# Output product of the first parity as seven half products, tiles that land in place, and places of their own for 130 tasks

## The chip, the cores and the metric

The kernel runs on one core of a Trainium2 chip. A core has TensorE (PE; its weight loads are listed as PEld), VectorE (DVE), ScalarE (ACT), GpSimd (POOL) and SyncE (SP), which here only issues DMA transfers. Each engine works through its own list of instructions in order. The metric is the time of one execution on the device in microseconds (us), the median of the runs; a profile is one execution of its own, taken with the hardware profiler.

## The reference

x has 2048 tokens of 640 numbers, all in float32. Two branches are mixed by a gate for each token: attention over 8 positions at distance 2 (32 heads of 20), and a dense layer with Mish.

```python
qkv = x @ wqkv                                   # 640 -> 3*640
logits = einsum("bhsd,bhswd->bhsw", q, kg) * DH**-0.5   # kg: k at s, s-2, ..., s-14
attn = softmax(where(mask, logits, -1e9))
o = einsum("bhsw,bhswd->bhsd", attn, vg)
a = o.reshape(B, S, 640) @ wo                    # the output product, 640 -> 640
h = x @ w1 + b1                                  # 640 -> 1728
b = (h * tanh(softplus(h))) @ w2                 # Mish, 1728 -> 640
g = sigmoid((x * gate_w).sum(-1, keepdims=True))
return g * a + (1 - g) * b
```

## The kernel before

**Tiles.** Everything is held transposed: features on the 128 partitions, 512 tokens along a row. The 2048 tokens are split by parity P (0, 1), and each parity into two blocks of 512, so tb = 0, 1 are the first parity and tb = 2, 3 the second. 640 features are five chunks (kc for those that are summed over, dc for those of the result).

**Precision.** A float32 tile becomes a pair of two fp32r tiles, a high part (ScalarE, line 400) and a low part, the difference (VectorE or GpSimd, line 403; `split`). A product of two pairs, `mm3` (lines 441 to 443), is three matmuls of 128x128 by 128x512. A tile is loaded into a staging buffer (rings `raw`, `hb`, `z`), then split into a buffer of the ring `pair` (`load_pair`).

**Half products.** A 2x2 block of products needs eight; the scheme of Strassen and Winograd does it in seven, with sums of the operands made ahead and sums of the results made behind. `quad` does the first layer of the MLP so: for two chunks of features and two token blocks, half products go into five PSUM banks, ScalarE copies one bank into another (line 887) as the start of the next sum, and VectorE closes (line 920). `mlp2` does the second layer with seven products a, b, c, e, g, d, f, each in seven steps over kc (step number 7k + kc for the k-th of them, 49 in all). The sums of w2 are made by `sums_of_w2` and kept in DRAM (s), the sums of activations by DMA with accumulation.

**Attention** is VectorE's work: eight units (parity by four groups of eight heads); products (lines 494, 532) and sums of 128x2560, softmax with ScalarE, and a transposed o of 128x640, which is stored to DRAM (`o<-ot`) and read again as chunks of 128 features.

**Output product** (`wo_out`, lines 1288 and after). For tb 0 and 1 the gated rows b of the MLP (`wo_row`, the gate's product on line 1127) are copied into a bank by ScalarE as its start (line 1274), five `mm3` over kc follow (`wo_bank`), ScalarE copies the bank out (line 1281), and the block is stored: 2 blocks x 5 dc x 5 kc x 3 = 150 matmuls. For tb 2 and 3 the first three kc come first, VectorE adds the result to b (line 1284), and the last two kc come at the end, again with a start and a copy by ScalarE. wo is loaded by `load_wo`, all of it, at step 26 of `mlp2`.

**What sets the order.** The program first records all work as tasks (`add`), each with an engine (or "ANY": VectorE or GpSimd), a duration, what it waits for, the buffers that it takes and holds, and a rank. `Plan.run` then plays them through and emits each engine's instructions in the order in which that play starts them: for each engine that is idle, of those tasks which are ready and whose buffers are free, the one with the lowest rank, then the earliest `need` (the place on TensorE of what waits for it, less `HOP` for each stage between), then the one recorded first. Rings hand out their buffers in the order of recording. FRONT lists the stages of the first part in the order in which they are recorded (Q units of qkv and attention, T quads, F and M rows of the first layer, S sums of w2, and the loads), BACK those which are recorded at a step of `mlp2` (2S5 is S with 5 at step 2; W is `load_wo`, G the gate's rows, P a row b). Loads of `mlp2` are recorded three steps ahead.

## Time and profile before

| | |
|---|---|
| time before, median of 3 runs | 624.56 us (624.12 to 627.35) |
| the profiled execution's own time | 628.4 us |
| its span | 626.3 us |
| mean granted clock of TensorE | 0.999 |
| DMA | 149.47 MB, mean 239 GB/s over the span |
| HBM read, written | 85.61 MB, 60.69 MB |

The span is what the profiler saw from the first to the last instruction; the execution's own time has some us around it. The stages by their places: the first layer and qkv until about 400 us, the seven products of the second layer from there to about 550, the output product to the end, with attention beside all of them until 580 us. Lines named "wait" give the engine, its line, what it waited for, the total, the number of times and the longest; rows of a timeline give start, duration, engine, line, operation, out<-in and, in brackets, idle time ahead and what ended it. Durations of matmuls are longer than their spacing, since they overlap. Names with a number less are tiles: `bank` PSUM, `pair`, `raw`, `hb`, `z` the rings, `kvq` rooms of attention of which some are reused, `act` and `actt` activations of the first layer in DRAM and their sums, `in_...` the inputs.

### The profile page before, as it was taken

To read this page: it belongs to the slowest core of one execution; us is meant where nothing else is said; L and a number is where in the kernel's file an instruction comes from. 1 tells how busy PE (TensorE), PEld (TensorE's weight loads), DVE (VectorE), ACT (ScalarE), POOL (GpSimd) and SP (SyncE) were. 2 spreads that over 40 slices of the span, in tenths; PEclk is the share of its full clock that TensorE was granted. 3 is DMA by queue.
4 is the path that set the end of the run, shared out by engine and by line. 5 is a ranking of instruction groups with operands and counts; after the bars stand their busy time and mean duration, and the time that the engine had idled before them with its cause. 6 is when DMAs were issued, how large, how long until landed. Compare 5 with 4: busy or idle time off the path is not lost.

```text
span 626.3 us, 8954 instructions
## 1 busy us (share of the span) xinstructions
PE 617.0 (99%) x2717; PEld 509.8 (81%) x2717; DVE 565.2 (90%) x581; ACT 384.2 (61%) x851; POOL 255.3 (41%) x250
## 2 busy tenths in 40 slices
PE   9999999998999999999999999989999999999997
PEld 6888888887888788888888888877888788888885
DVE  6899999998999999999999989989999999999630
ACT  6666765776496676766676535185858456575234
POOL 2563266546464445354456646441312431503000
PEclk9999999999999999999999999999999999999999
DMA  8866389998999699979997988689998687875404
GB/s 307 254 200 197 93 235 279 262 255 225 333 265 290 148 289 308 231 203 256 282 295 214 313 211 229 201 239 281 341 332 297 199 259 233 260 252 172 138 1 169
DMA packets 100609, 149.47 MB, mean 239 GB/s; under 512 B 11456, under 2 KB 47296, under 8 KB 100528
## 3 DMA queue, kind: packets, MB, share of 16 engines
q1 hardware_dynamic: 93456, 136.05, 67.6%
q0 software_dynamic: 7104, 12.85, 13.4%
q8 instruction: 21, 0.34, 0.2%
q14 instruction: 28, 0.23, 0.1%
HBM read 85.61 MB, written 60.69 MB: 234 GB/s over the span
## 4 chain that ended last, share of the span: by engine, by line
PE 87%; DVE 5%; DMA 4%; issue 2%; POOL 1%; ACT 1%; SPq 1%; DVEq 0%; POOLq 0%; ACTq 0%
PE bank L443 28%; PE bank L441 28%; PE bank L442 28%; DMA act<-z 1%; PE bank L587 1%; POOL pair L403 1%; DVE pr L494 1%; DVE pair L403 1%; DMA raw<-act 1%; PE bank L383 1%; PE bank L1208 1%; DMA hb<-act 1%; PE bank L1207 1%; DMA z<-act 0%; DVE pr L542 0%
## 5 line engine op out<-in xcount | busy, mean ns | idle before, releaser
L442 PE MATMUL bank<-pair 128*128 128x512 f32 (+2 forms) x812 | 314.8, 388 | 2.1 <-DVE pair L403 2.0
L441 PE MATMUL bank<-pair 128*128 128x512 f32 (+2 forms) x812 | 314.4, 387 | 0.0
L443 PE MATMUL bank<-pair 128*128 128x512 f32 (+2 forms) x812 | 314.3, 387 | 0.0
L403 POOL TENSOR_TENSOR pair<-raw,pair 128x512 fp32r<-128x512 f32 (+3 forms) x104 | 130.9, 1270 | 190.9 <-DVE side L536 47.3
L442 PEld LDWEIGHTS bank<-pair 128*128 128x128 f32 x812 | 152.5, 188 | 32.8 <-DVE pair L403 3.0
L441 PEld LDWEIGHTS bank<-pair 128*128 128x128 f32 x812 | 152.5, 188 | 30.6 <-ACT bank L887 0.5
L443 PEld LDWEIGHTS bank<-pair 128*128 128x128 f32 x812 | 152.6, 188 | 30.0 <-POOL pair L403 0.2
L400 ACT ACTIVATE pair<-raw 128x512 fp32r<-128x512 f32 (+3 forms) x198 | 117.0, 611 | 44.4 <-DMA raw<-act 19.7
L532 DVE TENSOR_TENSOR pr<-kvq,side 128x2560 f32<-128x2560 f32 x32 | 90.2, 2820 | 1.0
L497 DVE TENSOR_REDUCE lg<-pr 128x128 f32<-128x2560 f32 x32 | 90.1, 2817 | 0.7
L494 DVE TENSOR_TENSOR pr<-kvq,side 128x2560 f32<-128x2560 f32 x32 | 90.1, 2815 | 0.5
L403 DVE TENSOR_TENSOR pair<-raw,pair 128x512 fp32r<-128x512 f32 (+3 forms) x94 | 62.7, 690 | 7.3 <-ACT pair L400 7.0
L593 ACT ACTIVATE kvq<-bank 128x320 f32<-128x320 f32 x64 | 27.9, 437 | 46.8 <-PE bank L443 46.8
L542 DVE TENSOR_TENSOR pr<-pr 128x1280 f32<-128x1280 f32 x32 | 48.7, 1522 | 0.8
L400 ACT ACTIVATE pair<-hb 128x512 fp32r<-128x512 f32 (+2 forms) x40 | 24.7, 617 | 19.8 <-DMA hb<-actt 11.7
L403 POOL TENSOR_TENSOR pair<-hb,pair 128x512 fp32r<-128x512 f32 x12 | 15.6, 1301 | 42.3 <-PE bank L443 12.5
L887 ACT ACTIVATE bank<-bank 128x512 f32<-128x512 f32 x36 | 21.0, 584 | 16.0 <-PE bank L443 15.9
L441 PE MATMUL bank<-kvq,pair 128*128 128x512 f32 x72 | 28.3, 393 | 1.6 <-ACT bank L887 1.6
L443 PE MATMUL bank<-kvq,pair 128*128 128x512 f32 x72 | 28.3, 393 | 0.1
L442 PE MATMUL bank<-kvq,pair 128*128 128x512 f32 x72 | 28.1, 390 | 0.0
L740 POOL TENSOR_TENSOR raw<-raw 128x256 f32<-128x256 f32 (+1 forms) x24 | 20.4, 875 | 17.8 <-DVE side L536 8.2
L683 POOL DMA_DIRECT2D actt<-actt x26 | 22.4, 862 | 12.7 <-DVE pair L403 7.8
(125 smaller groups left out, 598.7 us busy)
## 6 DMA issues: line engine op xcount, KB each, us to landing
raw<-in_w SPq DMA_DIRECT2D x34, 256.0 KB, 4.8
raw<-actt SPq DMA_DIRECT2D x30, 256.0 KB, 4.0
raw<-in_wq SPq DMA_DIRECT2D x30, 248.0 KB, 3.5
raw<-in_x SPq DMA_DIRECT2D x29, 256.0 KB, 5.4
actt<-hb SPq DMA_DIRECT2D x28, 256.0 KB, 4.0
act<-z SPq DMA_DIRECT2D x24, 256.0 KB, 6.4
actt<-z SPq DMA_DIRECT2D x24, 256.0 KB, 6.0
raw<-act SPq DMA_DIRECT2D x23, 256.0 KB, 4.7
```

What stands on the lines that cost most here:

```text
L400: a = add("ACT", act_ns(n), lambda: A.activation(hi(), raw(), AF.Copy), after, rank=rank, take=take, hold=hold, kind="hi")
L403: return (V if e == "DVE" else G).tensor_tensor(lo(), raw(), hi().bitcast(F32), op=OP.subtract)
L441: nc.tensor.matmul(ps, ah, bh, start=first, stop=False, skip_group_check=more)
L442: nc.tensor.matmul(ps, ah, bl, start=False, stop=False, skip_group_check=more)
L443: nc.tensor.matmul(ps, al, bh, start=False, stop=last, skip_group_check=more)
L494: return V.tensor_tensor(pr, window(kv, s0, 0), qs[:, :, None, :].to_broadcast([128, 2, W, QF]), op=OP.mult)
L497: return V.tensor_reduce(lg_w[:, s0:s0 + 2], pr.rearrange("p s w (h d) -> p s w h d", d=DH), op=OP.add, axis=AX.X)
L532: return V.tensor_tensor(pr.rearrange("p s w (h d) -> p s w h d", d=DH), vw, pw[:, :, :, :, None].to_broadcast([128, 2, W, HQ, DH]), op=OP ...
L542: step("DVE", 1495, lambda: V.tensor_tensor(pr[:, :, 0:4], pr[:, :, 0:4], pr[:, :, 4:8], op=OP.add))
L593: a = add("ACT", 330, lambda: A.activation(kv[:, 7 + s], ps.t[:, QF:3 * QF].rearrange("p (a b) -> p a b", a=2), AF.Copy), [done] + before, ...
L683: return add("POOL", 1200, lambda: G.dma_start(out=blk[key][:rows], in_=src(), accum_op=OP.add, max_dma_last_dim=2048), after, rank=-0.5, ...
L887: return add("ACT", 590, lambda: A.activation(to.t, of.t, AF.Copy), after, rank=-0.6, take=[to], hold=[of], kind=kind)
```

## The change

1. *Output product of tb 0 and 1.* For dc = 0, 1 and dc = 2, 3 a new `wo_quad` does what `quad` does: 18 `mm3` with seven half products over kc 0 to 3 and the rest for kc 4, in place of 20; dc = 4 stays as it was. That is 46 `mm3` in place of 50, so 138 matmuls in place of 150. ScalarE copies banks three times in each quad; VectorE adds each of six bank results to its row b (`plus_bank`), where ScalarE made a start and a closing copy before.
2. *Sums ahead.* `sums_of_wo` (two times four sums of 128x256, three tiles stored) and `sums_of_o` (two times four sums of 128x512, four tiles stored) are recorded at steps 13, 21 and 23 of `mlp2`, kept in DRAM (`wt`, `os`) and loaded again for the quads. Three kinds of sums of o land in room of attention's `kvq0` after its unit 6 (`wo_sums`).
3. *Landing in place.* `Landing` with `inner=True` has a DMA write straight into the low half of a pair; ScalarE makes the high half from it, and the low half is overwritten by the difference. The activations and s of `mlp2`, o, os and wt land so.
4. *Rings and order.* `hb` has two buffers, `z` four. FRONT and BACK stand in another order; M for tb 2 and 3 is recorded at step 0, G at 35, and `load_wo` in three parts within `wo_out`. The constants of `Plan` change.
5. *Places of their own.* Five tables give single tasks, by their number, another key, a delay before they count as ready, another need, another rank, or one engine: 130 tasks in all.
6. *The host* lays wo out in blocks of 128 in the order of ORDER.

```diff
-SIZES = {"pair": 23, "home": 6, "raw": 9, "hb": 3, "z": 3}
+SIZES = {"pair": 23, "home": 6, "raw": 9, "hb": 2, "z": 4}
-BACK = "1M2 1M3 43P4 0S6 2S5 31P1 26W 22G 35P0"
-EARLY_S = 4000
+BACK = "23O0 13V0 0M2 7S6 21O1 2S5 35G 0M3 21V1"
+EARLY_S = 0
...
+HELD_BACK = """6:8079 17:633 18:4827 54:264 56:1872 184:656 185:632 187:1661 207:335 224:722 319:252 339:1148 354:778 384:1945
...
-    NEAR, TURN, PATIENCE, HOP, STAY, HELD = 4500, 2200, 11000, 3712, 3000, 24502
+    NEAR, TURN, PATIENCE, HOP, STAY, HELD = 3564, 1936, 11000, 6531, 3456, 14750
...
-            t.key = (t.rank, i)
+            t.key = (t.rank, i + moved.get(i, 0))
+            t.late += held.get(i, 0)
+            t.bias, t.only, t.turn = needed.get(i, 0), engine.get(i, 0), t.rank + ranked.get(i, 0)
...
-    def load_pair(src, eng, n=512, rank=SOON, drank=0.0, after=(), wide=False, home=None, cols=1):
-        raw, p = stage(wide), home or pair_buf()
+    class Landing:
+        def __init__(self, inner, n, home=None, wide=True):
+            self.p, self.n, self.inner = home or pair_buf(), n, inner
+            self.raw = None if inner else stage(wide)
+            self.take = [self.p if inner else self.raw]
...
+        def at(self, rows=slice(0, 128), a=0, b=None):
+            b = self.n if b is None else b
+            return self.p.t[rows, 1, a:b].bitcast(F32) if self.inner else self.raw.t[rows, a:b]
...
-        acts = [load_pair(lambda P=P: blk[of, P, kc], "ANY", wide=i > 2, after=done[of, P, kc]) for P in range(2)]
+        acts = [load_pair(lambda P=P: blk[of, P, kc], "ANY", after=done[of, P, kc], inner=True) for P in range(2)]
...
+    def sums_of_wo(m):
...
+        s1 = sum_into((r[2], 0), (r[1], 0), (r[0], 0), OP.subtract, [d0, d1], 256, take=[r[2]], rank=NEXT)
...
+        for i in (1, 2, 3):
+            wt_in[m, i] = [dma(lambda i=i: wt_d[m, i], lambda i=i: r[i].t, ends[i], rank=0.7, hold=[r[i]])]
+    def sums_of_o(kp):
...
+        s1 = sum_into((a22, 0), (a21, 0), (a22, 0), OP.add, a21.ready + a22.ready, 512, rank=NEXT)
+        s3 = sum_into((a21, 0), (a11, 0), (a21, 0), OP.subtract, [s1] + a11.ready, 512, rank=NEXT)
+        s2 = sum_into((a11, 0), (a22, 0), (a11, 0), OP.subtract, [s3], 512, rank=NEXT)
+        s4 = sum_into((a12, 0), (a12, 0), (a11, 0), OP.subtract, [s2] + a12.ready, 512, rank=NEXT)
+        for i, raw, t in ((1, a22, s1), (2, a11, s2), (4, a12, s4), (3, a21, s3)):
+            os_in[kp, i] = [dma(lambda i=i: os_d[kp, i], lambda raw=raw: raw.t, [t], rank=0.7, hold=[raw])]
...
+    def wo_quad(P, m, OX, OS, bs):
...
+        p1 = mm(one, of(xs(t0, 0), 0, 0), [], True, True, [one], "open")
+        p5 = mm(five, of(s(1), 2, 0), [p1], True, True, [five])
+        c2 = copy(two_, one, [p1])
+        plus_bank(t0, fb, five, [p5])
+        plus_bank(t1, fb, five, [p5])
+        p6 = mm(two_, of(s(2), 2, 256), [p5, c2])
+        p2 = mm(one, of(xs(t0, 1), 0, 256) + [(OX[t0, 4], R[3], 256)], [p6, c2], False, True)
+        plus_bank(t0, fa, one, [p2], True)
+        c3 = copy(three, two_, [p6])
+        p7 = mm(two_, of(s(3), 1, 0), [p2, c3])
+        c4 = copy(four, two_, [p7], "shut")
+        p3 = mm(three, of(s(4), 1, 256) + [(OX[t0, 4], R[3], 384)], [p7, c3], False, True)
+        plus_bank(t0, fb, three, [p3], True)
+        p4 = mm(two_, of(xs(t1, 1), 3, 0) + [(OX[t1, 4], R[3], 256)], [p3, c4], False, True)
+        plus_bank(t1, fa, two_, [p4], True)
+        p8 = mm(four, [(OX[t1, 4], R[3], 384)], [p4, c4], False, True)
+        plus_bank(t1, fb, four, [p8], True)
     def wo_out():
+        load_wo(0)
+        OX, OS = wo_sums(0)
+        load_wo(1)
+        bs = {(tb, dc): b for tb in (0, 1) for dc, b in enumerate(wo_rows(tb))}
+        for m in range(2):
+            wo_quad(0, m, OX, OS, bs)
+        load_wo(2)
+        OX.update({(1, kc): b for kc, b in wo_tokens(1, (0, 2)).items()})
         for tb in (0, 1):
-            ot = wo_tokens(tb, range(KC))
-            bs = wo_rows(tb)
-            for dc in range(KC):
-                wo_bank(tb, dc, bs[dc], ot, True, True)
+            wo_bank(tb, KC - 1, bs[tb, KC - 1], {kc: OX[tb, kc] for kc in range(KC)}, True, True)
```

The order of the instructions moves on every engine. Three places follow. The first is ScalarE in the quad that stands near 146 us of the profile before (hb and z are rows of Mish, lg the logits of attention). Before:

```order
L519 ACTIVATE lg_223<-lg_223 128x256
L400 ACTIVATE pair_1535<-raw_1441 128x512
L400 ACTIVATE pair_1545<-raw_1483 128x128
L695 ACT_TABLE_LOAD
L695 ACTIVATE hb_1547<-bank2_65,bias_77 128x512
L698 ACTIVATE hb_1547<-hb_1547 128x512
L887 ACTIVATE bank6_69<-bank3_66 128x512
```

And after the change:

```order
L576 ACTIVATE lg_223<-lg_223 128x256
L752 ACT_TABLE_LOAD
L752 ACTIVATE hb_1556<-bank3_66,bias_77 128x512
L752 ACTIVATE z_1550<-z_1550,bias_77 128x512
L439 ACTIVATE pair_1569<-raw_1398 128x512
L944 ACTIVATE bank6_69<-bank5_68 128x512
L439 ACTIVATE pair_1582<-raw_1416 128x128
```

The split of 128x128 stood ahead of the table load, the Mish and the bank copy, and stands behind them now; one of the two other splits stands between Mish and copy.

The second place is SyncE's list at the first steps of the second layer (act21 are activations of product b, h2 and h3 the last rows of the first layer on their way through DRAM, s5 and s6 sums of w2). Before:

```order
L409 DMA h2_196<-pair_3833 32x2x128
L409 DMA h2_196<-pair_3833 32x2x128
L409 DMA h3_197<-pair_3840 32x2x128
L409 DMA h3_197<-pair_3840 32x2x128
L409 DMA raw_3896<-act11_1_6_98 128x512
L409 DMA s5_188<-raw_3823 128x128
L409 DMA hb_3899<-act21_0_2_101 128x512
L409 DMA pair_3833<-h2_196 64x512
L409 DMA raw_3915<-act21_0_0_99 128x512
```

(The eight stores stand in one block; the last two of each four are shown.) And after:

```order
L448 DMA pair_3919<-act21_0_2_101 128x512
L448 DMA pair_3922<-act21_1_2_108 128x512
L448 DMA h2_196<-pair_3844 32x2x128
L1050 DMA hb_3928<-in_w2 64x384
L1050 DMA hb_3928<-in_w2 64x384
L448 DMA s6_189<-raw_3842 128x128
L448 DMA h2_196<-pair_3844 32x2x128
L448 DMA s5_188<-raw_3597 128x128
L448 DMA h2_196<-pair_3844 32x2x128
L448 DMA pair_3963<-act21_0_3_102 128x512
L448 DMA pair_3967<-act21_1_3_109 128x512
```

The eight stores are spread between loads, most of product b's activations stand ahead of the later ones, and they go into pair buffers.

The third place is SyncE's list within product c (actt2 are its activations, s its weights, o attention's result, b a finished row of the MLP). Before:

```order
L409 DMA raw_4235<-actt2_1_3_151 128x512
L409 DMA raw_4249<-actt2_0_4_145 128x512
L409 DMA raw_4257<-actt2_1_4_152 128x512
L1025 DMA hb_4259<-s4_187 128x256
L1025 DMA hb_4259<-s5_188 128x256
L409 DMA raw_4269<-actt2_1_5_153 128x512
```

And after:

```order
L448 DMA raw_4212<-o0_190 128x512
L1078 DMA pair_4225<-s4_187 128x256
L1078 DMA pair_4225<-s5_188 128x256
L448 DMA wt0_2_247<-raw_4080 128x512
L448 DMA pair_4244<-actt2_0_4_145 128x512
L448 DMA pair_4247<-actt2_1_4_152 128x512
L448 DMA pair_4262<-actt2_0_5_146 128x512
L448 DMA pair_4270<-actt2_1_5_153 128x512
L448 DMA raw_4275<-o1_191 128x512
```

Loads of o and a store of a sum of wo now stand between the loads of product c; that store waits for VectorE's sum, and the loads of steps 4 and 5 stand behind it.

More of the change, by code (lines that the diff above doesn't have):

```diff
@@ L38 @@
 KEPT = "".split()
+DEEP = 3
 AHEAD = 1.0
@@ L177, in run @@
                         continue
-                    t = min(fit, key=(lambda t: (t.rank, t.need if t.need is not None and e in ("DVE", "POOL", "ACT") and self.ORDERED else 1e9, t.key)))
+                    t = min(fit, key=(lambda t: (t.turn, (t.need if t.need is not None and e in ("DVE", "POOL", "ACT") and self.ORDERED else 1e9) + t.bias,
+                                            t.key[1])))
                     if t.both:
@@ L996, in load_low_w @@
[L996 to L1003 removed]
+                nc.sync.dma_start(to.at(slice(a, a + FR)), src())
@@ L1377 @@
     mlp2(mid, listed)
-    if not WO:
-        load_wo()
     wo_out()
```

242 lines of the change are left out of this document (178 added, 64 removed), and 15 rows, old and new, of tables (HELD_BACK, NEEDED, RANKED).

## The prediction

> **What bounds the kernel now.** First the page's first part, the busy time of each engine. One line carries it:
>
> ```profile
> PE 617.0 (99%) x2717; PEld 509.8 (81%) x2717; DVE 565.2 (90%) x581; ACT 384.2 (61%) x851; POOL 255.3 (41%) x250
> ```
>
> TensorE is busy 99% of the span, so a matmul that goes away is worth its spacing. A busy row is longer than that spacing, since matmuls overlap; it is read from the timeline, from two starts that stand 90 matmuls apart:
>
> ```profile
> 509.40 0.39 PE L441 MATMUL bank<-pair 128*128 128x512 f32 x1
> 529.80 0.39 PE L441 MATMUL bank<-pair 128*128 128x512 f32 x1
> ```
>
> 20.40/90 = 0.2267 us each, at a granted clock of 1.00. Second, the waits of TensorE:
>
> ```profile
> PE bank L442 <- DVE pair L403: 2.0, 1, 2.0
> PE bank L441 <- ACT bank L887: 1.6, 1, 1.6
> PE bank L383 <- DVE lg L379: 1.2, 1, 1.2
> PE bank L1208 <- DVE pair L1013: 0.2, 1, 0.2
> ```
>
> That is all: 5.0 us, and 1.2 of it is the start. After a gap the next matmuls also start slowly; the chain of the end has six more such pieces outside the two long waits, with 0.40 to 0.50 where 0.23 is usual, first and last:
>
> ```profile
> 179.17 0.50 PE bank L441
> 501.39 0.47 PE bank L1208
> ```
>
> They hold about 1.5 us together (six times about 0.25). Third, who feeds TensorE. The windows give, after the stretch and its length, the busy time of PE, PEld, DVE, ACT and POOL, then the clock, the busy share of the DMA engines and GB/s:
>
> ```profile
> 430.00:480.00 50.00, 50.00 (x222) 41.43 (x221) 48.16 (x63) 35.77 (x74) 9.12 (x8) 1.00 1.02 334
> 430.00:580.00 150.00, 149.74 (x660) 123.56 (x659) 146.00 (x184) 95.86 (x194) 38.63 (x33) 1.00 0.82 264
> 580.00:610.00 30.00, 30.00 (x134) 24.86 (x133) 13.99 (x22) 8.32 (x14) 0.00 (x0) 1.00 0.22 68
> ```
>
> VectorE has only 150 − 146.0 = 4.0 us free in the 150 us from 430, yet TensorE waits 0.26 us there. From 430 to 480 the DMA engines are full as well. From 580 VectorE has 30 − 14.0 = 16 us to spare. So **TensorE bounds, with VectorE right behind it**, and any forecast is a question of whether VectorE can take more.
>
> **The sum.** All terms are made on the profiled execution, 628.4 us (span 626.3, and 2.1 around it); it lies 3.8 above the median of 624.56, with the same clock. I take it that the differences carry over, so the forecast on the profile's scale is 3.8 higher.
>
> 1. *Twelve matmuls go.* Two quads of 18 half or single products stand for two times 20 in tb 0 and 1; 46 products of three matmuls in place of 50. 12 × 0.2267 = **−2.7**. This is the surest term.
>
> 2. *The wait at 146 us.* ScalarE's timeline:
>
> ```profile
> 143.10 0.31 ACT L400 ACTIVATE pair<-raw 128x128 fp32r<-128x128 f32 x1 [2.34 <-DMA raw<-in_w]
> 143.43 1.28 ACT L695 ACT_TABLE_LOAD   x1
> 144.73 0.69 ACT L695 ACTIVATE hb<-bank,bias 128x512 f32<-128x512 f32 x1
> 145.98 0.58 ACT L887 ACTIVATE bank<-bank 128x512 f32<-128x512 f32 x1
> 146.61 0.50 PE L441 MATMUL bank<-kvq,pair 128*128 128x512 f32 x1 [1.59 <-ACT bank L887]
> ```
>
> (The last row is TensorE's.) A small split waits 2.34 us for its weights at the head of ScalarE's in-order queue; behind it stand a table load, the Mish and the bank copy that TensorE needs. In the new order this split stands behind the bank copy, and the table load and the Mish need not wait for it. The copy then comes up to 2.34 us earlier, more than the 1.59 that TensorE lost: **−1.6**. Next late there: the Mish needs a free hb buffer, of which there are two in place of three, so it waits for an earlier store.
>
> 3. *The wait at 411 us.* Four engines carry it:
>
> ```profile
> 395.98 5.60 SPq L409 DMA_DIRECT2D h<-pair  x8
> 403.69 0.53 SPq L409 DMA_DIRECT2D raw<-act  x1
> 408.11 0.63 ACT L400 ACTIVATE pair<-raw 128x512 fp32r<-128x512 f32 x1 [2.16 <-DMA raw<-act]
> 409.70 0.56 DVE L978 SCALAR_TENSOR_TENSOR pair<-raw,pair 128x384 fp32r<-128x384 f32 x1 [2.72 <-ACT pair L977]
> 412.44 0.69 DVE L403 TENSOR_TENSOR pair<-hb,pair 128x512 fp32r<-128x512 f32 x1
> 413.78 0.50 PE L442 MATMUL bank<-pair 128*128 128x512 f32 x1 [1.98 <-DVE pair L403]
> ```
>
> Eight stores of the last rows of mlp1 hold SyncE's queue for 5.60 us; the loads behind them are issued late (403.69), ScalarE splits late, VectorE stands idle for 2.72 us and then works off a heap. In the new order the activations of product b are issued ahead of these stores and between them, straight into pair buffers: **−2.0**. What is late next are the stores themselves, and their loads back: the last rows of mlp1 now come between the loads of product b, and a load that stands behind a store waits 0.7 us (5.60/8), not 5.6.
>
> 4. *Six more bank copies by ScalarE.* They stand on TensorE's path in a quad. The price of such copies so far:
>
> ```profile
> L887 ACT ACTIVATE bank<-bank 128x512 f32<-128x512 f32 x36 | 21.0, 584 | 16.0 <-PE bank L443 15.9
> ```
>
> 36 copies and one wait of 1.6 us: 6/36 × 1.6 = **+0.3**; bounds 0 (each hidden behind the next half product) and 6 × 0.58 = 3.5. ScalarE itself, with 61%, loses the seeds and closing copies of tb 0 and 1; two more table loads (1.28 each, above) are hidden there.
>
> 5. *VectorE's added work.* By the counts of instructions it has 18 more of 128x512, 6 more of 128x256 and two fewer of 128x384. Their prices:
>
> ```profile
> 557.95 1.29 DVE L1127 TENSOR_TENSOR kvq<-kvq,pair 128x512 f32<-128x512 f32 x2
> 559.16 0.69 DVE L403 TENSOR_TENSOR pair<-z,pair 128x512 fp32r<-128x512 f32 x1
> L960 DVE TENSOR_TENSOR raw<-raw 128x256 f32<-128x256 f32 x5 | 2.1, 411 | 0.0
> ```
>
> Start to start a 512 costs (559.16 − 557.95)/2 = 0.605, so 18 × 0.605 + 6 × 0.411 − 2 × 0.56 (the row at 409.70) = 12.2 us. About 6.3 of it are early sums in products c to g (seven of 512 by 0.605, five of 256 by 0.411); most of the rest are the twelve closings. Cover: the 4.0 us free from 430 to 580, the 2.72 at 409.70, and 16 us after 580. Attention would finish some 5.5 us later (12.2 − 6.7), which the 16 can hold. Bounds 0 and 12.2. I take **+0.5**, a quarter of the one wait for VectorE of 2.0 that the kernel shows, since the early sums have no due time at TensorE and can be put behind the splits; but the sums' stores can't be put behind: SyncE waits for a sum with a store of wt at the head of its queue, and behind it stand activations of product c.
>
> 6. *More transfers in the full stage.* Between the first load of product c and that of g there are 11 more transfers of 256 KB (five stores of wt, three loads and one store of o and its sums, two loads of wo), 2.88 MB; at 334 GB/s (row 430 to 480) 8.6 us. For it: gate rows and most of wo are loaded later than before, and tiles landing in place are asked for earlier. Bounds 0 and 8.6; I take one of the eleven as late, 8.6/11 = **+0.8**, nearer to 0 because the row shows all 222 matmuls in 50 us without a pause although the share is 1.02 already. The Trainium skill, "DMA: Bandwidth & Descriptors", section "Where 436 GB/s comes from", puts the limit between HBM and one core at about 358 GB/s and that of the fabric at 435; by the second this term would be nothing, by the first the upper bound would be an estimated 8.1 us. That 334 comes with a share of 1.02 speaks for the first. What is late next is wo itself: its loads now fall between 480 and 580, where the DMA engines have been busy for 0.72 of the time:
>
> ```profile
> 480.00:580.00 100.00, 99.74 (x440) 82.13 (x439) 97.85 (x122) 60.08 (x121) 29.51 (x26) 1.00 0.72 229
> ```
>
> So there is room for them: 28 us of full transfer in these 100 us.
>
> 7. *Landing in place itself* moves no work between engines: the same splits, read from the pair's low half. Its price is that a pair buffer is held through the transfer; 0, hidden by the three steps of loads ahead, else part of 6. The sums of o land in kvq0, whose room is free only when attention's seventh unit has ended; if VectorE is late, so are they, which is again B.
>
> Sum: −2.7 − 1.6 − 2.0 + 0.3 + 0.5 + 0.8 = −4.7, **619.9 us** (623.7 on the profile's scale).
>
> **The rivals.**
>
> *B: VectorE takes over as the pace.* Its free 6.7 us are used, the other 5.5 are on TensorE's path because splits come behind sums and closings: −2.7 − 3.6 + 0.3 + 5.5 = −0.5, **624.1**. For it: 146 of 150 us busy. Against it: what is added is not itself needed soon, and attention can slip into the 16 us. Here it also falls if the waits of 2 and 3 only move. It decides against a gain of 0.5% from 2.9 us unhidden on.
>
> *C: slower, by late transfers at the head of VectorE's queue.* In products c and e the eleven transfers make tiles late; VectorE works in order, so each late tile stops all behind it, its spare time is lost to such waits, and all of the 12.2 are on the path: −6.0 + 12.2 = +6.2, **630.8**. It decides from 9.1 us unhidden (6.0 + 3.1). For it: the share of 1.02, and the 2.72 us at 409.70, which are such a wait. Against it: no wait of TensorE from 430 to 480.
>
> *D: VectorE and GpSimd in each other's way.* The rows:
>
> ```profile
> L403 DVE TENSOR_TENSOR pair<-raw,pair 128x512 fp32r<-128x512 f32 x75 | 50.7, 695 | 5.5 <-ACT pair L400 5.2
> L403 DVE TENSOR_TENSOR kvq<-raw,kvq 128x512 fp32r<-128x512 f32 x5 | 6.4, 1280 | 0.1
> ```
>
> The same split took 1280 ns in five cases, 585 more. GpSimd gets 14 more elementwise operations of 512; if each held up one of VectorE's, 14 × 0.585 = 8.2 on top of B: −0.5 + 8.2 = +7.7, **632.3**. The mean of 695 over 75 says that the order mostly keeps them apart. The Trainium skill, "SBUF — State Buffer", section "Who interferes with whom", says that only the port pair which these two share causes contention, as an exclusive lock; the 1280 agrees, the 695 shows it avoided.
>
> **How the numbers follow.** About 0.5% (3.1 us: 621.4 and 627.7) is what a measurement here can tell from no change. Forecast 0.56, the only case that is faster; B 0.27, the same; C 0.14 and D 0.03, slower. The low end: terms 4 to 6 at nothing (−1.6), the 0.2 of L1208 and the 1.5 of slow starts gone, gives 616.6, and 0.4 for the fastest run's distance from the median: 616.2. The high end: B with the 2.7 us at 409.70 not won back for VectorE, 626.8. C and D, 0.17, are left out.
>
> **What would show it.** In the changed profile: 2705 matmuls or so; no wait for a bank copy of 1.6 near 146 us; no wait for VectorE near 411; DVE's 128x512 operations still near 690 ns; VectorE's last attention product near 584 in place of 578, with the last matmul 4.7 us earlier. B shows as several waits of TensorE for splits by VectorE between 430 and 580; C as VectorE idle behind ScalarE and DMA in products c and e; D as a mean far above 690. The forecast is wrong if the waits of TensorE, 5.0 us now, do not fall below about 3.

## The result, and the profile after

The changed kernel takes **640.87 us** (median of 6 runs, 637.57 to 642.00); the kernel before took 624.34 us beside it (6 runs, 623.56 to 627.35). The ratio is **1.0233, 95% interval 1.0209 to 1.0258**: slower, where 619.9 was forecast and 626.8 was the upper end. The profiled execution took 641.11 us, with a span of 639.4 and a mean granted clock of 0.991 (before 628.4, 626.3 and 0.999).

The page's busy times:

```profile
PE 619.5 (97%) x2705; PEld 509.5 (80%) x2705; DVE 586.5 (92%) x602; ACT 388.6 (61%) x855; POOL 291.6 (46%) x269
```

The twelve matmuls are gone (2705), yet TensorE's share fell from 99% to 97%: it waits. VectorE is busy for 21.3 us more, GpSimd for 36.3 us more (19 more instructions). The waits of TensorE, as total, times and longest:

```profile
PE bank L499 <- POOL pair L442: 6.0, 1, 6.0
PE bank L498 <- ACT kvq L1156: 2.6, 1, 2.6
PE bank L500 <- DVE pair L442: 1.5, 2, 0.9
PE bank L422 <- DVE lg L418: 1.2, 1, 1.2
...
PE bank L500 <- POOL pair L442: 0.9, 1, 0.9
...
PE bank L498 <- ACT bank L944: 0.7, 2, 0.4
```

The two long waits of before (2.0 for a split by VectorE, 1.6 for ScalarE's bank copy) are not among them. In their place stand one of 6.0 us for a split by *GpSimd* and one of 2.6 us for ScalarE's bank copies. The windows (busy time of PE, PEld, DVE, ACT and POOL, then clock, DMA share, GB/s) say where:

```profile
430.00:480.00 50.00, 50.00 (x222) 41.43 (x221) 48.20 (x58) 32.33 (x63) 18.20 (x18) 1.00 0.97 325
480.00:550.00 70.00, 70.00 (x311) 57.89 (x310) 68.22 (x78) 43.94 (x86) 28.95 (x23) 1.00 0.94 307
560.00:570.00 10.00, 4.01 (x13) 2.95 (x12) 6.27 (x11) 2.64 (x6) 8.62 (x2) 0.79 0.91 330
580.00:610.00 30.00, 30.00 (x134) 24.68 (x133) 29.14 (x41) 10.34 (x19) 5.12 (x4) 1.00 0.55 178
```

From 430 to 550, where the prediction looked for trouble, TensorE runs without a pause beside full DMA engines and a VectorE that is busy for 116.4 of 120 us. Then, from 560 to 570, it does 13 matmuls in place of 44, GpSimd is busy for 8.62 us with two instructions, and the clock falls to 0.79.

**The stall at 561.** The timelines of VectorE, GpSimd and TensorE there (start, duration, engine, line, operation):

```profile
556.56 1.88 DVE L442 TENSOR_TENSOR pair<-pair 128x512 fp32r<-128x512 f32 x3
...
564.98 1.29 DVE L442 TENSOR_TENSOR kvq<-kvq 128x512 fp32r<-128x512 f32 x2
572.54 0.69 DVE L1466 TENSOR_TENSOR z<-bank,z 128x512 f32<-128x512 f32 x1 [6.27 <-PE bank L500]
...
559.62 9.01 POOL L442 TENSOR_TENSOR pair<-pair 128x512 fp32r<-128x512 f32 x2 [18.93 <-DMA o<-ot]
...
561.07 0.39 PE L498 MATMUL bank<-pair 128*128 128x512 f32 x1
567.44 0.79 PE L499 MATMUL bank<-pair 128*128 128x512 f32 x1 [5.99 <-POOL pair L442]
568.03 0.63 PE L500 MATMUL bank<-pair 128*128 128x512 f32 x1
568.46 0.63 PE L498 MATMUL bank<-pair 128*128 128x512 f32 x1
568.89 0.63 PE L499 MATMUL bank<-pair 128*128 128x512 f32 x1
```

From 556.56 to 566.27 VectorE runs a train without a gap: sixteen operations, all with both operands in SBUF (the memory that holds the tiles, beside PSUM with its banks), one every 0.605 us. GpSimd begins a split of 128x512 in the middle of it, at 559.62. Such a split lies at about 1.3 us elsewhere; this one ends at 567.39 (it is the first of the two in the row, 7.78 us by the chain), 1.12 us after the train. It is as if GpSimd had stood still until VectorE let go. TensorE needs this split and waits 5.99 us; VectorE, at the end of its train, then waits 6.27 us for TensorE. And after the wait TensorE's matmuls start 0.43 us apart in place of 0.23, for some 5 us.

**The wait at 418.** ScalarE, then TensorE:

```profile
417.98 1.28 ACT L752 ACT_TABLE_LOAD   x1
419.28 0.72 ACT L752 ACTIVATE pair<-pair,bias 64x512 f32<-64x512 f32 x1
420.03 0.63 ACT L755 ACTIVATE pair<-pair 64x512 f32<-64x512 f32 x1
420.56 2.02 ACT L1156 ACTIVATE kvq<-bank 128x512 f32<-128x512 f32 x4
...
421.19 0.50 PE L498 MATMUL bank<-pair 128*128 128x512 f32 x1 [2.60 <-ACT kvq L1156]
...
424.13 0.63 PE L498 MATMUL bank<-pair 128*128 128x512 f32 x1
424.55 0.63 PE L499 MATMUL bank<-pair 128*128 128x512 f32 x1
```

Product a is done at 418.6, and its banks must be copied out before product b's next sum can begin. Ahead of those copies on ScalarE stands the Mish of the last 64 rows of the first layer, with a table load: 2.6 us. These rows came back from DRAM late, since their eight stores now lie between loads:

```profile
406.51 0.32 SPq L448 DMA_DIRECT2D h<-pair  x1
...
411.24 1.58 SPq L448 DMA_DIRECT2D h<-pair  x3
...
413.97 1.14 SPq L448 DMA_DIRECT2D pair<-h  x2
```

**By stretches.** The table takes, from the matmuls' start times, all distance between neighbours beyond 0.2267 us; so it holds waits and slow matmuls together (us; early matmuls of 496 or 498 columns stand closer, hence the negative sums).

| | 0–12 | 12–145 | 145–300 | 300–430 | 430–480 | 480–550 | 550–580 | 580–end | sum |
|---|---|---|---|---|---|---|---|---|---|
| before | 2.9 | −1.4 | 1.3 | 1.4 | 0 | 0.7 | 0 | 0 | 4.9 |
| after | 3.4 | 1.1 | 1.6 | 4.3 | 0 | 0 | 10.4 | 0.2 | 20.9 |

The difference of 16.0, less 2.7 for twelve matmuls, is 13.3; the span grew by 13.1, since what follows the last matmul became 0.2 us shorter. (The medians stand 16.5 apart and the ratio gives 14.5; the profiled execution of before, with 628.4 us, lay above all six runs.) 10.4 of it lies between 550 and 580: the wait of 6.0 at 561, the slow matmuls behind it, and a wait of 1.1 at 557 whose cause the trace does not name.

### The profile page after: what moved, and what is told of

It is laid out like the page before. It is cut to its first block, busy times and chain, and to the rows that moved or that the text cites. A ratio compares the mean times of both kernels' runs of the same rounds, so it can differ in the third digit from the quotient of the medians.

```text
span 639.4 us, 9048 instructions
## 1 busy us (share of the span) xinstructions
PE 619.5 (97%) x2705; PEld 509.5 (80%) x2705; DVE 586.5 (92%) x602; ACT 388.6 (61%) x855; POOL 291.6 (46%) x269
## 3 DMA queue, kind: packets, MB, share of 16 engines
q0 software_dynamic: 7104, 12.85, 13.3%
## 4 chain that ended last, share of the span: by engine, by line
PE 51%; DVE 9%; DMA 3%; issue 1%; POOL 1%; ACT 1%; SPq 1%; DVEq 0%; POOLq 0%; ACTq 0%
PE bank L499 17%; PE bank L500 17%; PE bank L498 17%; DVE lg L554 2%; DVE pr L551 2%; DVE pr L589 1%; DMA pair<-act 1%; POOL pair L442 1%; DVE pr L599 1%; SPq L448 1%; DMA s<-raw 1%; PE bank L1258 1%; PE bank L1257 0%; DMA pair<-h 0%; DVE pr L600 0%
## 5 line engine op out<-in xcount | busy, mean ns | idle before, releaser
L499 PE MATMUL bank<-pair 128*128 128x512 f32 (+2 forms) x796 | 309.9, 389 | 6.0 <-POOL pair L442 6.0
L498 PE MATMUL bank<-pair 128*128 128x512 f32 (+2 forms) x796 | 309.3, 389 | 3.8 <-ACT kvq L1156 2.6
L500 PE MATMUL bank<-pair 128*128 128x512 f32 (+2 forms) x796 | 309.3, 389 | 0.9 <-POOL pair L442 0.9
L499 PEld LDWEIGHTS bank<-pair 128*128 128x128 f32 x796 | 150.1, 189 | 36.9 <-POOL pair L442 6.9
L498 PEld LDWEIGHTS bank<-pair 128*128 128x128 f32 x796 | 149.9, 188 | 34.8 <-ACT kvq L1156 3.0
L500 PEld LDWEIGHTS bank<-pair 128*128 128x128 f32 x796 | 150.2, 189 | 31.0 <-POOL pair L442 1.3
L442 POOL TENSOR_TENSOR pair<-raw,pair 128x512 fp32r<-128x512 f32 (+4 forms) x78 | 99.2, 1285 | 105.9 <-ACT pair L439 32.3
L442 POOL TENSOR_TENSOR pair<-pair 128x512 fp32r<-128x512 f32 (+2 forms) x56 | 80.0, 1440 | 123.0 <-ACT pair L439 40.7
L439 ACT ACTIVATE pair<-pair 128x512 fp32r<-128x512 f32 (+1 forms) x147 | 85.0, 615 | 63.3 <-DMA pair<-act 28.7
L439 ACT ACTIVATE pair<-raw 128x512 fp32r<-128x512 f32 (+3 forms) x118 | 68.1, 607 | 14.1 <-DMA raw<-in_x 5.8
L442 DVE TENSOR_TENSOR pair<-pair 128x512 fp32r<-128x512 f32 (+1 forms) x91 | 59.3, 691 | 1.6 <-ACT pair L439 1.6
L599 DVE TENSOR_TENSOR pr<-pr 128x1280 f32<-128x1280 f32 x32 | 52.4, 1637 | 0.7
L797 POOL TENSOR_TENSOR raw<-raw 128x256 f32<-128x256 f32 (+1 forms) x29 | 26.8, 931 | 22.0 <-DVE pr L551 5.6
L500 PE MATMUL bank<-kvq,pair 128*128 128x512 f32 x84 | 33.5, 399 | 1.5 <-DVE pair L442 1.5
L498 PE MATMUL bank<-kvq,pair 128*128 128x512 f32 x84 | 33.8, 402 | 0.2 <-ACT bank L944 0.2
L499 PE MATMUL bank<-kvq,pair 128*128 128x512 f32 x84 | 33.4, 397 | 0.4 <-DVE kvq L442 0.4
L442 DVE TENSOR_TENSOR pair<-raw,pair 128x512 fp32r<-128x512 f32 (+4 forms) x40 | 27.1, 698 | 6.5 <-ACT pair L439 6.3
```

The lines of the kernel that those rows point to most:

```text
L439: a = add("ACT", act_ns(n), lambda: A.activation(hi(), raw(), AF.Copy), after, rank=rank, take=take, hold=hold, kind="hi")
L442: return (V if e == "DVE" else G).tensor_tensor(lo(), raw(), hi().bitcast(F32), op=OP.subtract)
L498: nc.tensor.matmul(ps, ah, bh, start=first, stop=False, skip_group_check=more)
L499: nc.tensor.matmul(ps, ah, bl, start=False, stop=False, skip_group_check=more)
L500: nc.tensor.matmul(ps, al, bh, start=False, stop=last, skip_group_check=more)
L599: step("DVE", 1495, lambda: V.tensor_tensor(pr[:, :, 0:4], pr[:, :, 0:4], pr[:, :, 4:8], op=OP.add))
```

## The experiments

Two theories at the outset. *Train*: two splits that the tables put on GpSimd inside a train of VectorE cost most of it. *Place*: the new order is too tight as a whole, and any split would be late there. Each ratio is to runs of the kernel before, made beside it on the same chip.

**x1: does a train of VectorE hold GpSimd?** A program of its own that leaves out the whole computation: GpSimd adds 128x512 tiles in SBUF, first alone, then beside trains of VectorE that begin at the same time.

> A small kernel by itself, it leaves the whole computation out: three GpSimd additions of 128x512 beside (a) nothing, (b) 12 and (c) 24 VectorE additions of 128x512 from SBUF back to back, (d) 12 with one operand in PSUM, (e) 12 reductions of one operand, (f) 8 additions and 8 reductions in turn, then (a) and (c) again. Theory 'lock': a GpSimd addition cannot get in between VectorE additions that follow one another without a gap, so the first one lasts until the train ends: about 1.3 us in (a), 12 x 0.605 = 7.3 us or so in (b), 14.5 us in (c), 1.3 us in (d) and (e), 1.3 to 2.6 us in (f). Rival 'shared bandwidth': both slow down, GpSimd to about 2.6 us and VectorE's additions to about 1.2 us, whatever the length of the train.

Timeline, the three adds alone and beside 24 adds of VectorE:

```profile
12.43 3.70 POOL L34 TENSOR_TENSOR gb<-ga,gb 128x512 f32<-128x512 f32 x3
...
27.11 17.73 DVE L47 TENSOR_TENSOR vc<-va,vb 128x512 f32<-128x512 f32 x24
27.21 0.64 POOL L38 COPY ga<-gate 128x8 f32<-128x8 f32 x1 [4.38 <-DVE gate L30]
27.93 4.93 POOL L34 TENSOR_TENSOR gb<-ga,gb 128x512 f32<-128x512 f32 x3
```

The train began 0.10 us before GpSimd's first operation (a small copy) and 0.82 us before its first add. Still GpSimd got in after the operation of VectorE that was then running, and from there the two took turns: 1.64 us an add in place of 1.23, while VectorE's train took 17.73 us for 24 × 0.605 = 14.5. No lock for the whole train, so the theory fell in this form. Beside operations with one operand, or one in PSUM, GpSimd kept its 3.7 us.

**x2: the two splits back on VectorE**, all else by the same tables.

```diff
-ENGINE = """54:2 68:2 ... 2098:1"""
+ENGINE = """54:2 68:2 ... 2098:1 2477:1 2501:1"""
```

> The changed kernel, with two low-half splits of tiles of the output product's first quad (tasks 2477 and 2501, which GpSimd took at 559.6 us and needed 7.8 us for the first) fixed on VectorE. Theory 'lock': the wait of 6.0 us and most of the slow clock behind it go; TensorE's excess over even spacing from 550 to 580 us falls from 10.4 to 2 to 4 us and the time from 640.9 to 632 to 635. Rival 'VectorE is behind': the tiles are late anyway, TensorE waits at the same place for VectorE, over 4 us; time 637 or more.

632.07 us (7 runs), ratio 1.0099 [1.0067, 1.0131]: 8.8 us faster than the changed kernel by the medians. The window of the stall:

```profile
550.00:580.00 30.00, 30.00 (x133) 24.50 (x132) 29.97 (x51) 17.85 (x34) 5.30 (x2) 1.00 0.73 245
```

TensorE has no pause left there (0.3 us in the table's measure, 10.4 before), although VectorE is busy for 29.97 of 30 us: it had the time for both splits. So *train* holds for this stretch, and *place* does not.

Up to 560 us the order of every engine is the same in both programs, and yet their traces differ there. The wait for ScalarE's bank copies is 0.8 us in this one, at 424, and at 408 stands one that the changed kernel's trace does not have:

```profile
PE bank L499 <- DVE pair L442: 2.9, 1, 2.9
```

From 300 to 430 us this execution loses 6.7 us, that of the changed kernel 4.3. So a wait of 2 or 3 us in one trace can be missing in another execution of the same order.

**x3: the planner's guard restored.** Plan lets GpSimd work beside VectorE's long attention products only if its operation ends with them, or if the task's rank is negative. The tables lower the rank of 2477 by 2.25 and of 2501 by 0.5, and the guard reads the lowered one.

```diff
-    fit = [t for t in fit if now + t.ns[0] <= quiet + 150 or t.turn < 0]
+    fit = [t for t in fit if now + t.ns[0] <= quiet + 150 or t.rank < 0]
```

> The changed kernel, where GpSimd's rule (elementwise work only beside VectorE's long attention products) is waived by a task's recorded rank again, and not by the rank that the table RANKED gives it. Theory 'lock': the table's negative ranks let GpSimd in beside VectorE's two-operand work; without that, GpSimd operations of over 1.5 us fall from 18 to about 7 as before the change, VectorE's sums of 128x1280 from 1637 ns back to about 1522, and the time is 626 to 633. Rival 'VectorE has too much to do': the splits fall to VectorE instead, its backlog grows, and the time is 638 or more.

639.00 us (4 runs), ratio 1.0207 [1.0162, 1.0253]: a miss. GpSimd's operations of over 1.5 us fell from 18 to 10, VectorE's sums of 128x1280 from 1637 to 1489 ns, and the stall at 561 went, but the whole order was played out anew, and new waits stand at 436 to 467:

```profile
PE bank L498 <- ACT pair L439: 6.0, 1, 6.0
PE bank L499 <- DVE pair L442: 4.7, 2, 3.1
```

The table's numbers are fitted to one play of the plan; change a rule and they place other instructions badly. Its time says nothing on GpSimd's cost.

**x4 and x11: no tables.** The rest of the change as it is; the same program, measured twice.

```diff
-        moved, held, needed, ranked, engine = map(table, (MOVED, HELD_BACK, NEEDED, RANKED, ENGINE))
+        moved, held, needed, ranked, engine = map(table, ("", "", "", "", ""))
```

> The changed kernel with the five tables empty: quads, landing in place, rings, order strings and constants stay. Theory 'the tables do the harm' (through GpSimd beside VectorE): 622 to 632, GpSimd's mean for a split in place near 1300 ns. Rival 'the structure does the harm' (more work for VectorE, fuller DMA): 640 or more, with waits for VectorE in the seven products and in the quads.

> The changed kernel without the tables once more, beside the run before it on the same chip: 626 to 629, and the spread of single runs, by which the two are compared.

627.47 us, ratio 1.0021 [0.9991, 1.0051], and 627.74 us, ratio 1.0031 [1.0011, 1.0052], 10 runs each. The tables are thus about 2.1 of the 2.33 per cent. GpSimd has 7 elementwise operations of over 1.5 us, as before the change, in place of 18. One long wait is left, that at 418, here in x4:

```profile
PE bank L498 <- ACT kvq L1156: 4.5, 1, 4.5
```

In x11 it is 3.8 us, in x10 and x12, whose order is the same up to 550 us, 3.1 and 2.7. With the tables it was 2.6 in the one trace, so they made no clear difference to it.

**x5: a GpSimd operation that comes in the middle of a train.** As x1 (the computation left out), but GpSimd's add waits for the sixth of VectorE's 18 operations.

> A small kernel by itself again, with the whole computation left out. In the first one GpSimd asked when a train of VectorE began, and the two took turns. Here GpSimd's addition waits for the sixth of 18 VectorE operations, so that it asks in the middle of a train: (a) 18 additions from SBUF, (b) the same with three GpSimd additions, (c) 18 subtractions in place on pairs, (d) and (e) one operation with an operand in PSUM, or one reduction, as the 13th, (f) all 18 with an operand in PSUM. Theory 'a running train is not broken': in (a) to (c) the first GpSimd addition lasts until the train ends, 12 x 0.605 + 1.2 = 8.5 us, with VectorE's operations not lengthened; in (d) and (e) it gets in at the 13th, about 5 us; in (f) 1.2 us. Rival 'turns': about 1.6 us in (a) to (e) with one or two VectorE operations lengthened; then the 7.8 us at 559.6 has another cause.

Timeline: a plain train, a train with one operation that reads PSUM, and a train of such operations alone:

```profile
26.84 10.92 DVE L33 TENSOR_TENSOR vc<-va,vb 128x512 f32<-128x512 f32 x18
30.62 8.27 POOL L49 TENSOR_TENSOR gb<-vc,ga 128x512 f32<-128x512 f32 x1 [29.78 <-DVE vc L33]
...
70.55 4.59 POOL L49 TENSOR_TENSOR gb<-vc,ga 128x512 f32<-128x512 f32 x1 [4.03 <-DVE vc L33]
73.93 0.68 DVE L40 TENSOR_TENSOR vc<-bank,vb 128x512 f32<-128x512 f32 x1
...
93.43 1.26 POOL L49 TENSOR_TENSOR gb<-vc,ga 128x512 f32<-128x512 f32 x1 [6.24 <-DVE vc L40]
```

Here is the stall by itself. One add of 1.26 us took 8.27 (8.19 and 8.20 in the two other trains without a break): the train ends at 37.76, the add 1.12 us later, the very distance seen at 566. One operation with an operand in PSUM let it in earlier (4.59; a reduction did the same, 4.59); the train of those did not touch it. The train itself was not lengthened (18 × 0.605 = 10.9). So whether GpSimd is let in depends on when it comes: within the first operation of the train, and the two take turns (x1); after the sixth, and it stands until the train has a gap. What decides between the two, no run shows. The Trainium skill, "SBUF — State Buffer", section "SBUF: two separate sides", has the side that starts first hold the shared pair of ports for its whole instruction while the other blocks. By that the add would have waited one operation, 0.6 us; the measured 8.27, some twelve operations, decides. That operations of VectorE with at most one SBUF input do not contend, as section "Who interferes with whom" of the same page of the Trainium skill has it, these runs show too (1.26 us here, 3.71 and 3.72 for three adds in x1).

**x10 and x12: one split put on GpSimd in an order that has no stall.** The order of x4, with one task near 553 (x10) or 556 us (x12) emitted on GpSimd.

```diff
-                    ins = t.fn(e) if t.both else t.fn()
+                    ins = t.fn("POOL" if self.tasks.index(t) == 2480 else e) if t.both else t.fn()
```

> The changed kernel without the tables, with one instruction moved and the order kept otherwise: the split of the tile that stalled the changed kernel at 561 us, which VectorE makes here at 554.6 us within a train of operations from SBUF, goes to GpSimd. Theory 'a running train is not broken': GpSimd's split begins near 555, lasts until the train's gap at 561 us, some 7 us, TensorE waits for it 4 us or more and starts slowly behind it, and the time is 5 to 9 us above the same kernel without this move (x11). Rival 'it was the tables' order as a whole': within 2 us of it.

> The changed kernel without the tables again, with one instruction moved from VectorE to GpSimd and the order kept otherwise. In x10 the moved split found a gap of 0.3 us in VectorE's train and got in. This time it is the next split of the same product (task 2480), whose high half is ready at 555.6 us, in the middle of a train without a gap until about 560.5. Theory 'a running train is not broken': GpSimd's split lasts from 555.6 to about 561.5, 5 to 6 us in place of 1.3; TensorE, which takes the tile at 556.5 or so, waits 3 to 5 us, starts slowly behind it, and the excess from 550 to 580 us rises from 0.3 to between 4 and 8; the time 4 to 8 us above x11, 631 to 636. Rival 'chance of the order': excess and time stay within 2 us of x11.

x10 (task 2477): 627.88 us (10 runs), ratio 1.0045 [1.0010, 1.0080], no difference from x11 by the medians. (Two of the ten, 632.60 and 633.83, lie above all runs of x11; they have no trace.) In the profiled execution the split took 2.19 us, not the rest of the train, since the train had a gap:

```profile
553.41 2.19 POOL L442 TENSOR_TENSOR pair<-pair 128x512 fp32r<-128x512 f32 x1 [14.74 <-ACT pair L439]
...
554.75 1.41 DVE L442 TENSOR_TENSOR pair<-pair 128x512 fp32r<-128x512 f32 x1 [0.30 <-ACT pair L439]
```

0.30 us free were enough for GpSimd to get in, and then VectorE's split was the one held (1.41 in place of 0.68). The expectation missed because the train was not gapless. x12 (task 2480): 630.40 us (9 runs), ratio 1.0089 [1.0060, 1.0117], 2.7 us above x11 by the medians and 3.6 by the ratios, less than expected. The mechanism is the expected one:

```profile
556.35 5.63 POOL L442 TENSOR_TENSOR pair<-pair 128x512 fp32r<-128x512 f32 x1 [16.09 <-PE bank L1257]
...
558.37 2.49 DVE L442 TENSOR_TENSOR pair<-pair 128x512 fp32r<-128x512 f32 x4
...
562.03 0.80 PE L499 MATMUL bank<-pair 128*128 128x512 f32 x1 [3.48 <-POOL pair L442]
```

VectorE's train ends at 560.86, GpSimd's split at 561.98, and from 550 to 580 TensorE lost 5.4 us in the profiled execution (633.97 us, the second longest of the nine). The nine runs lie between 628.93 and 634.83; why its price varies so was not looked into.

**x6 and x9: the wait at 418.** Both start from x4. x6 sends the last rows' stores ahead of the loads, and the plan, played anew, changes the order in many other places too; x9 keeps x4's order and puts only the two Mish tasks of these rows, with their stores, behind the four bank copies.

```diff
 x6, in turned_out:
-                    after, rank=1.0, hold=hold, size=81920, late=late) for g in range(4)]
+                    after, rank=-1.0, hold=hold, size=81920, late=late) for g in range(4)]
 x9, where tasks are emitted:
+                    if k in (1754, 1755, 1756, 1757):
+                        stash.append(t)
...
+                    if k == 1867:
+                        for u in stash:
+                            u.fn()
```

> The changed kernel without the tables, and with SyncE's stores of the last rows of the first layer ahead of other transfers (rank -1 in place of 1). Without the tables TensorE has one long wait left, 4.5 us at 418 us for ScalarE's copies of banks, which stand behind these rows' table load and Mish. Theory 'late rows': the rows come back earlier, their Mish is done before the banks are free, the wait falls below 1 us, the excess of 300 to 430 us from 5.9 to under 2 and the time from 627.5 to 622 to 625. Rival 'the stores only change places with loads': a wait for a split of product b, 2 us or more as before the change, and the time 626 or more.

> The changed kernel without the tables, its order kept instruction by instruction but for one place: the table load and the Mish of one block of the first layer's last rows, which stand ahead of ScalarE's four copies of product a's banks at 415 us, stand behind them (and two of their stores behind two loads of o). Theory 'the Mish holds up the copies': TensorE's wait of 4.5 us at 418 us falls below 0.7 us, the excess of 300 to 430 us from 5.9 to about 1, and the time from 627.5 to 622 to 623.5, below the kernel before. Rival 'the banks are not free earlier' or 'the rows of the Mish are then late': 626 or more, the wait standing elsewhere.

Both took the wait away, and neither gained: x6 630.94 us (4 runs), ratio 1.0103 [1.0059, 1.0147]; x9 628.40 us (12 runs), 1.0050 [1.0028, 1.0073]. In x6 the loss moved to 454 and 457 (6.8 us from 430 to 480, none in x4), in x9 to 432.7. The waits of x6, then that of x9 (its lines are 9 higher):

```profile
PE bank L499 <- DVE pair L442: 2.8, 3, 2.2
PE bank L498 <- ACT pair L439: 2.0, 1, 2.0
```

```profile
PE bank L508 <- POOL pair L451: 2.1, 1, 2.1
```

In x9 that split was due at 430.5, and its tile was not late: ScalarE had made its high half by 419.7. The low half was GpSimd's, which stood idle for 6.66 us until VectorE had finished line 611, and VectorE had itself stood idle for 1.97 us for another tile:

```profile
428.97 1.95 DVE L451 TENSOR_TENSOR pair<-pair 128x512 fp32r<-128x512 f32 x3 [1.97 <-ACT pair L448]
...
431.40 2.53 POOL L451 TENSOR_TENSOR pair<-pair 128x512 fp32r<-128x512 f32 x2 [6.66 <-DVE kvq L611]
```

The plan ties such an operation of GpSimd to the last operation of VectorE ahead of a long attention product (`follow` in `Plan.run`). So what comes next there is the order of the splits. This trace is of the shortest of the twelve runs (624.52 us); what the longer runs lose, it does not show.

**x7: landing in place undone** (from x4; staging buffers as before, in all places, nine lines; one is shown).

```diff
-        acts = [load_pair(lambda P=P: blk[of, P, kc], "ANY", after=done[of, P, kc], inner=True) for P in range(2)]
+        acts = [load_pair(lambda P=P: blk[of, P, kc], "ANY", wide=i > 2, after=done[of, P, kc]) for P in range(2)]
```

> The changed kernel without the tables, and with landing in place undone: all tiles land in raw, hb or z and are split from there. Theory 'landing in place brings earlier loads': without it loads wait for staging buffers, TensorE waits for splits in the seven products, time 630 or more. Rival 'landing in place is neutral': within 2 us of 627.5.

661.37 us (4 runs), ratio 1.0574 [1.0533, 1.0615]. TensorE's waits:

```profile
PE bank L498 <- ACT pair L439: 12.3, 6, 6.5
PE bank L499 <- DVE pair L442: 8.3, 8, 2.1
PE bank L499 <- POOL pair L442: 6.1, 2, 3.7
```

Nearly all stand between 430 and 550. In this order, with o, os and wt asked for beside the products and two buffers in `hb` and four in `z`, 34 us hang on landing in place. It does not say what it would bring to the order of before.

**x8: the old output product** (from x4, with 150 matmuls, its starts and closing copies, no sums ahead).

```diff
-BACK = "23O0 13V0 0M2 7S6 21O1 2S5 35G 0M3 21V1"
+BACK = "0M2 7S6 2S5 26W 35G 0M3"
...
-        for m in range(2):
-            wo_quad(0, m, OX, OS, bs)
...
+            for dc in range(KC):
+                wo_bank(tb, dc, bs[dc], ot, True, True)
```

> The changed kernel without the tables, and with the output product of tb 0 and 1 as it was, 150 matmuls, no sums of wo and o, wo loaded at step 26. Theory 'the quads bring their twelve matmuls': 2.7 us more, 630.2. Rival 'VectorE and DMA pay for them': 627.5 or less, VectorE's busy time some 12 us lower.

630.30 us (4 runs), ratio 1.0084 [1.0054, 1.0114]. Against x4 the quads gain 2.8 us by the medians, 0.6% by the ratios, while VectorE is busy for 580.5 us with them and 559.8 without: 21 us more on the fullest feeder, and in neither run did TensorE lose more than 0.4 us after 430.

No version that was run is faster than the kernel before.

## Why the prediction was wrong

The 2.33% (14.5 us of 624.34) split so, by the ratios: 1.34 points (8.4 us; 8.8 by the medians) are two splits on GpSimd inside a train, shown by x2; about 0.73 points (4.6 us) the rest of the tables, by the difference of x2 and x4 with x11; 0.26 points (1.6 us) the change without tables, by x4 and x11. The ratios are uncertain by 0.2 to 0.3 points each, so the two smaller parts are rough. For the 4.6 us no run names a cause. By the measure of the stretches, the changed kernel and x2 lose 2.7 and 2.8 us between 12 and 300, the four traces without tables (x4, x10, x11, x12) −0.6 to 1.0, so about half of it lies there. The trace of the changed kernel has more of VectorE and GpSimd in each other's way early on (line 599 takes 1637 ns on the mean where the same line took 1522, line 602 581 in place of 490) and small waits between 77 and 311; that is a reading, not a test.

1. *Twelve matmuls, −2.7: right.* 2705 matmuls; x8 gives 2.8, net of what the quads cost elsewhere.
2. *The wait at 146, −1.6: right.* The bank copy stands ahead of the small split, and ScalarE waits for TensorE there and not the reverse:

```profile
146.68 0.58 ACT L944 ACTIVATE bank<-bank 128x512 f32<-128x512 f32 x1 [0.39 <-PE bank L500]
147.17 0.31 ACT L439 ACTIVATE pair<-raw 128x128 fp32r<-128x128 f32 x1
```

3. *The wait at 411, −2.0: wrong.* It is gone in the changed kernel's trace (in x2, of the same order, 2.9 us stand at 408), but the step asked only how long a load stands behind a store ("a load that stands behind a store waits 0.7 us, not 5.6") and not who waits for the stored rows. They came back 9 to 11 us later (loads at 413.97, before at 403.09 and 404.79). Their table load and Mish stood ahead of ScalarE's bank copies before too, but were over by 413; now they fell where the copies were due: 2.6 us of wait with the tables, 2.7 to 4.5 without, and slow matmuls behind most of these. From 300 to 430 the loss rose from 1.4 to 4.3 us (6.7 in x2, 5.9 in x4) where it was to vanish, so the term is +3 or more. x6 and x9 show that this is no lone fault: with it gone, splits behind it are late.
4. *Six bank copies, +0.3: right.* No wait for them in the trace; 0.7 us for those of line 944.
5. *VectorE's added work, +0.5: right in the stretch it spoke of, and B falls.* VectorE is busy for 21 us more with the quads than without (x4, x8), against 12.2 counted; splits that either engine may do can have changed sides. Yet from 430 to 550 no time is lost; after 580 it is busy for 29.1 of 30 us, in the room that the prediction named.
6. *Eleven transfers, +0.8: nothing.* Share 0.97, 325 GB/s, all 222 matmuls in 50 us; C falls with it.
7. *Landing in place, 0: not neutral.* The new order stands on it (x7, 34 us). What its price is, a pair held through the transfer, no run shows.

**The step that failed** is the one that was not there: part 5 of the change, places for 130 tasks, got no term, so it stood at nothing without a reason. In its place the runs show 2.1 of the 2.33 points, about 13 us: 8.4 for two splits on GpSimd inside a train and 4.6 for the rest of the tables. And the rival nearest to what happened was weighed by the wrong trace. D had VectorE lengthened by 0.585 us for each of 14 operations, 8.2 in all, with a chance of 0.03, because "the mean of 695 over 75 says that the order mostly keeps them apart". That mean is of the order before; it cannot vouch for an order that tables have rewritten. The 0.585 is itself a mean over held and free splits: in the trace of before three of the five took 1.61 to 1.78 us and two 0.68. The direction was wrong too: in the stall VectorE was not held up, GpSimd was, once, for 7.78 us in place of 1.3, with TensorE behind it. D's own sign, a mean far above 690, did not show: in the changed kernel VectorE's splits of 128x512 take 706 ns over 83 and 683 over 26. That D's 8.2 lies near the 8.4 of the two splits is chance. The sign could have been doubted ahead: the tables name tasks 2477 and 2501 with lowered ranks, and the plan counts 1329 ns for GpSimd's split, whatever VectorE does.

One premise was weak besides: that differences of the profiled execution carry over to the median. That execution lay 3.8 us above the median at the same clock, and the two waits that terms 2 and 3 were to win back make up 3.6 us of it. A median run can then hardly have had both, so part of the 3.6 was not there to win. No trace of a shorter execution of before shows which.

## What to carry to other kernels

A split that TensorE waits for does not go to GpSimd while VectorE runs two-operand SBUF work without a gap: leave it to VectorE, or see that a gap or an operation with one SBUF operand comes in time. Price a table of places like any other part of a change: build the new order, and look on each row it moves for what stands beside it now, since a mean from the old order says nothing of it. Where a wait is taken out by moving stores or loads, follow the data that moved to the one who reads it. And before a wait of one trace is booked as a gain, ask whether that execution was a typical one.

## What the runs showed of the hardware

An operation of GpSimd that came into the middle of a running train of VectorE stood until the train's gap (7.78, 5.63 and 8.27 us for 1.3 us of work, each ending 1.12 us after the train). A gap of 0.30 us let it in (x10), and so did one operation with a single SBUF operand (x5). When GpSimd asked 0.10 us after the start of the train's first operation, it got in and the two took turns (x1).

TensorE's matmuls started 0.43 us apart, at half the usual rate and a granted clock of 0.50, for 2.7 to 5.3 us after waits of 2.07 (x9), 2.60, 3.48 (x12) and 5.99 us. Waits of 1.59 and 1.98 us in the kernel before were not followed by that, and neither were waits of 2.40 and 2.67 us in x12. In the changed kernel the slow stretch after the 2.60 us began only 1.3 us behind the wait. The Trainium skill, "TensorE: Matmul & The Clock Gate", section "What's actually happening", has the clock halved after an idle window of about 3.4 us that runs freely. Here 2.07 us of idleness were enough once and 2.67 us were not another time, so a wait shorter than the Trainium skill lets one expect can be followed by slow matmuls, and its length alone does not tell.
